# Two column groups instead of one by seven block products in the first channel mixing of batches 2 to 6, six output buffers instead of eight, and a written-out order for every engine

## The chip, the cores and the metric

The kernel runs on one core of a Trainium2 chip. A core has a matrix engine (TensorE, "PE" in the profile; its weight loads are shown apart as "PEld"), a vector engine (VectorE, "DVE"), an engine for activations (ScalarE, "ACT"), a general engine (GpSimd, "POOL") and an engine that here only issues transfers (SyncE, "SP"). Each runs its own list of instructions in order; an instruction that waits for another engine or for a transfer holds up everything behind it on its engine. Products land in PSUM, eight banks of 128 x 512 fp32, from which only DVE and ACT read.

The metric is device time in microseconds, the median of several runs. Before the change it is 247.42 us (three runs, 247.22 to 247.65).

## The reference: what is computed

There are 8 batches of 576 positions, 8 heads of 64, in fp32. Linear attention comes first, and its output, 576 x 512 per batch, goes into a mixer with four weights:

```python
phi = where(x > 0, x, exp(x) - 1) + 1            # applied to q and k
kv  = einsum('bhsd,bhse->bhde', phi(k), v);  z = phi(k).sum(seq)
x   = (phi(q) @ kv) / (phi(q) . z + 1e-6)        # 576 x 512 per batch
h   = relu(x.T @ w_tok1) @ w_tok2                # token mixing, 576 -> 256 -> 576
u   = x + h.T
out = u + relu(u @ w_ch1) @ w_ch2                # channel mixing, 512 -> 1536 -> 512
```

The channel mixing is most of the arithmetic: two products of 576 x 512 x 1536 per batch.

## The kernel before

**Tiles.** The 576 positions of a batch are four row tiles of 128 and a tail of 64; the tails of two batches are mixed together. Work is in bf16, sums and outputs in fp32. The steps of a batch, with their lines: `load` (L132) brings two head pairs of q, k or v (576 KB) into a raw buffer; from batch 2 on there is one raw buffer per tensor. `phi_exp` (L151, ACT), `phi_add` (L157, DVE) and `phi_end` (L165, DVE, a min of the two) make phi; `vcast` (L176) casts v. `kv` (L191) is the k-v product, `nd_all` (L261 on PE, L270 to L289 on DVE) the numerators and denominators. `mm1` (L312) and `mm2` (L325, residual on DVE in L337) are the token mixing. Transposes by DMA (L221 for q, L521 and L526 for u) are issued from SP.

**First channel mixing.** Twelve column groups of 128, each one PSUM bank: `mm3` (L543) makes four products of 512 columns, and ACT applies the Relu (L550; DVE in a few, L547). Groups 4, 5, 10 and 11 of batches 2 to 6 go another way: `mix_one` takes their 512 x 512 block product as seven products of half-size blocks (Strassen's scheme in Winograd's form) instead of eight, each as four products of 256 columns (L712). It needs sums of the weight blocks (`group_sums`, once, L700) and of the blocks of u (`u_sums`, DVE, L689, per batch). Three of the seven are copied out by ACT (L720), three are read by DVE as add-and-Relu (L531), one by ACT as Relu (L718). Batch 7 does all its groups this way (`mix_first`, L740, L746, L748).

**Second channel mixing.** For batches 1 to 6 `pair_product` (L852) makes seven half-size products, after row sums of the first mixing's result (`row_sums`, L655, DVE). `pair_copy` (L857, ACT), `pair_end` (L861 on DVE, L863 on POOL) and `pair_put` (L867) put an output together in four slots of `obuf`, of which there are eight, taken in rotation. Batch 0 uses `mm4` (L583).

**What sets the order.** Each engine runs its instructions in the order in which the code makes them. `run(big, fill)` calls a list of PE steps (`big`: first mixing, second mixing) and, after each, the steps of the next batches that were put at that place by hand (`fill`). So attention and token mixing of batch n+1 lie between the products of batch n, and phi of batch n+2 beside them. PSUM banks come from two rotating rings or from small tables in the functions. SP's order of loads and transposes follows from the same places. A load can be gated on another transfer (`after`): k of batch 1 waits for the first quarter of the first channel weights, the second quarter of the second channel weights waits for the first half of q of batch 1, and q of batch 2 for that quarter. Weights come on POOL's queue.

Of the kernel before, what the change touches and what calls it, by code (L numbers as in the profile page):

```python
# [10 lines left out]
FP32 = mybir.dt.float32  # L11
# [4 lines left out]
EPS = 1e-6  # L16


@with_exitstack
def kernel(  # L20
# [20 lines left out]
    nc = tc.nc  # L41
# [22 lines left out]
    ring = {1: 0, 2: 0}  # L64

    def bank(at=None):
        if at is None:
            at, ring[1] = ring[1], (ring[1] + 1) % 4
        return psum[:, at]

    def banks(at=None):
        if at is None:
            at, ring[2] = 4 + ring[2], (ring[2] + 2) % 4
        return psum[:, at:at + 2]

    def two16():
        return banks().bitcast(BF16).rearrange("p a (t s) -> p a t s", s=128)
# [24 lines left out]
    uTj = [t.rearrange("p r j c -> p (r j c)").rearrange("p (j r c) -> p j r c", j=NDM, r=R) for t in uT]  # L102
    uTt = const("uTt", [128, 2, NDM, 128])
    cr = [const(f"cr{b}", [128, NCH, SM]) for b in range(2)]
    crt = const("crt", [128, NCH, 128])
    obuf = const("obuf", [128, 8, DM], FP32)
    swc = const("swc", [128, 4, 2, 256])
# [31 lines left out]

    live = {}  # L140
    o_at = [0]

    def o_slots(m):
        at = o_at[0] if o_at[0] + m <= 8 else 0
        o_at[0] = (at + m) % 8
        return obuf[:, at:at + m]

    def phi_exp(nm, n, j0, nj):
        f = raw[nm, rb(n)][:, j0:j0 + nj].rearrange("p j f -> p (j f)")
        e = work.tile([128, 2 * TD], BF16, name="e", tag="e", bufs=4)[:, :nj * TD]  # L150
        nc.scalar.activation(out=e, in_=f, func=AF.Exp)  # L151
        live["e", nm, n, j0] = e

    def phi_add(nm, n, j0, nj):
        f = raw[nm, rb(n)][:, j0:j0 + nj].rearrange("p j f -> p (j f)")
        y = work.tile([128, 2 * TD], BF16, name="y", tag="y")[:, :nj * TD]
        nc.vector.tensor_scalar(out=y, in0=f, scalar1=1.0, scalar2=1.0, op0=ALU.add, op1=ALU.max)  # L157
        for j in range(nj):
            live["y", j0 + j] = y[:, j * TD:]

    def phi_end(nm, n, j0, nj):
        c, i = divmod(j0, 2)
        dst = (kp if nm == "k" else qp)[:, c, :, i:i + nj]
        e, y = live["e", nm, n, j0], live["y", j0][:, :nj * TD]
        live["phi"] = nc.vector.tensor_tensor(  # L165
            out=dst.transpose([0, 2, 1, 3]), in0=e.rearrange("p (i t d) -> p i t d", i=nj, t=T),
            in1=y.rearrange("p (i t d) -> p i t d", i=nj, t=T), op=ALU.min)

    def phi(nm, n, c):
        phi_exp(nm, n, 2 * c, 2)  # L170
        phi_add(nm, n, 2 * c, 2)
        phi_end(nm, n, 2 * c, 2)

    def vcast(n, c, copy=nc.scalar.copy):
        js = slice(2 * c, 2 * c + 2)
        copy(out=vs[:, js, :, 0:D],  # L176
             in_=raw["v", rb(n)][:, js].rearrange("p j (t d) -> p j t d", t=T))

    def bank16():
        return bank().bitcast(BF16).rearrange("p (t s) -> p t s", s=128)  # L180
# [3 lines left out]
    def kv(n, cs):  # L184
        b = n % 2
        ps = banks(4 if n > 1 else None)[:, :, 0:2 * D1].rearrange(
            "p a (c e) -> p a c e", c=2)
        for c in cs:
            for t in range(T):
                for a, i in QUARTERS:  # L190
                    nc.tensor.matmul(out=ps[half[i], a, c], lhsT=kp[half[a], c, t, i],  # L191
                                     rhs=vs[half[a], 2 * c + i, t],
                                     start=(t == 0), stop=(t == T - 1))
        cs = slice(cs[0], cs[-1] + 1)
        for i in range(2):
            at = slice(i * D1, (i + 1) * D1)
            nc.scalar.copy(out=kvbd[b][half[i], cs, :, at].transpose([0, 2, 1, 3]),
                           in_=ps[half[i], :, cs])
# [6 lines left out]
    TS = [range(0, 5), range(5, T)]  # L205

    def qtr_put(n, c, ts, tp, put, dst=None):
        v_ = (qT[n % 2] if dst is None else dst)[:, 0:4 * TD].rearrange("p (a c t s) -> p a c t s", a=2, c=2, t=T)
        put(out=v_[:, :, c, ts[0]:ts[-1] + 1].transpose([0, 2, 1, 3]),
            in_=tp[:, 0:len(ts)].rearrange("p t (a s) -> p t a s", a=2))  # L210

    def qtr(n, c, put=nc.scalar.copy):
        tp = two16()
        for h, ts in enumerate(TS):
            qtr_mm(c, ts, tp[:, h])
        for h, ts in enumerate(TS):
            qtr_put(n, c, ts, tp[:, h], put)

    def qtr_dma(n, halves=range(2)):
        for a in halves:  # L220
            live["crossbar"] = nc.sync.dma_start_transpose(  # L221
                out=qT[n % 2][:, 2 * TD * a:2 * TD * (a + 1)].rearrange("p (f s) -> p f s", s=D),
                in_=qp[half[a]].rearrange("p c t i d -> p (c t i d)"))

    def nd_mm(n, c, rs):
        b = n % 2
        ps = banks()
        for s_, r in enumerate(rs):
# [5 lines left out]
        live["nd", c, rs[0]] = ps  # L234

    def nd_end(n, g, rs):
        b = n % 2
        m = len(rs)
        v_ = live["nd", g, rs[0]][:, 0:m, 0:HG * D1].rearrange("p r (h e) -> p r h e", h=HG)
# [9 lines left out]

    def nd_all(n):
        b = n % 2
        ps = [psum[:, 2 + 2 * m:4 + 2 * m] for m in range(3)]
# [10 lines left out]
        xv = x[b].rearrange("p r (c i a d) -> p i (r c) a d", c=2, i=2, a=2)  # L265
        v_ = [ps[m][:, :, 0:D1 * 7].rearrange("p i (k e) -> p i k e", k=7) for m in range(3)]
        dens = work.tile([128, 2, 2, 7], FP32, name="dens", tag="dens", bufs=1)
        last = work.tile([128, 2, 6], FP32, name="dens2", tag="dens2", bufs=1)
        both = psum[:, 2:6, 0:D1 * 7].rearrange("p b (k e) -> p b k e", k=7)
# [4 lines left out]
        def six(m, k0, rc0):  # L274
            den = (dens[:, m] if m < 2 else last)[:, :, k0:k0 + 6]
            nc.vector.tensor_tensor(  # L276
                out=xv[:, :, rc0:rc0 + 3],
                in0=v_[m][:, :, k0:k0 + 6, 0:D].rearrange("p i (q a) d -> p i q a d", a=2),
                in1=den.rearrange("p i (q a) -> p i q a", a=2)[
                    :, :, :, :, None].to_broadcast([128, 2, 3, 2, D]), op=ALU.mult)  # L280

        for m, at in enumerate((6, 0)):
            six(m, m, 4 * m)
            nc.vector.tensor_tensor(
                out=xv[:, :, 3, m], in0=v_[m][:, :, at, 0:D],
                in1=dens[:, m, :, at, None].to_broadcast([128, 2, D]), op=ALU.mult)
        nc.vector.tensor_scalar(out=last, in0=v_[2][:, :, 0:6, D], scalar1=EPS, scalar2=None,
                                op0=ALU.add)
        nc.vector.reciprocal(out=last, in_=last)  # L289
        six(2, 0, 7)  # L290

    def nd(n, g, rs):
        nd_mm(n, g, rs)
        nd_end(n, g, rs)

    ALL = slice(0, DM)
# [9 lines left out]
    def mm1(n):  # L306
        b = n % 2
        ps = banks(4 if n > 1 else None)
        for mt in range(NT):
            ms = slice(128 * mt, 128 * mt + 128)  # L310
            for r in range(R1):
                nc.tensor.matmul(out=ps[:, mt], lhsT=w1t[:, b, ms] if r == R else w1[:, r, ms],  # L312
                                 rhs=x[b][:, r, :], start=(r == 0), stop=(r == R))
        for mt in range(NT):
            nc.scalar.activation(out=ar[b][:, mt, :], in_=ps[:, mt], func=AF.Relu)

    def mm2(n, rs, add=False):

        b = n % 2
        m = len(rs)  # L320
        ps = bank().rearrange("p (a d) -> p a d", a=1) if n == 1 else banks(
            None if n < 2 else 4 if rs[0] else 6)
        for i, r in enumerate(rs):
            for kt in range(NT):
                nc.tensor.matmul(out=ps[:, i], lhsT=w2v(kt, r, b),  # L325
                                 rhs=ar[b][:, kt, :], start=(kt == 0),
                                 stop=(kt == NT - 1 and not add))
            if add:
                nc.tensor.matmul(out=ps[:, i], lhsT=identity, rhs=x[b][:, r, :], start=False,
                                 stop=True)  # L330
        if rs[0] == R:
            h = half[b]
            nc.vector.tensor_tensor(out=ut[n // 2 % 2][h], in0=ps[h, 0], in1=x[b][h, R], op=ALU.add)
        elif add:
            nc.scalar.copy(out=u[b][:, rs[0]:rs[0] + m], in_=ps[:, 0:m])
        else:
            nc.vector.tensor_tensor(out=u[b][:, rs[0]:rs[0] + m], in0=ps[:, 0:m],  # L337
                                    in1=x[b][:, rs[0]:rs[0] + m], op=ALU.add)

    def mm2_tails(p):  # L340

        ps = banks(6)[:, 0]
        for kt in range(NT):
            at = D * (T * kt + 2 * R)
# [966 lines left out]
```

## Time and profile before

| | before |
|---|---|
| median of the runs | 247.42 us |
| profiled execution, first to last instruction | 246.4 us |
| PE busy | 236.1 us (96%) |
| DVE busy | 198.8 us (81%) |
| ACT busy | 139.3 us (57%) |
| POOL busy | 76.9 us (31%) |
| granted PE clock | full in all of the span |

The profiled execution is one run; its span stands 1.0 us below the median of the timed runs. The page counts matmuls as busy from start to modelled end, so that neighbours overlap: what one costs is the distance between starts in the chain of work, not its mean length. A group row reads "line engine operation, out<-in, shapes, count | busy us, mean ns | idle before it, and what ended that idle time". Rows of waits read "engine line <- what it waited for: us in total, times, longest". A row of stages reads from:to, length, then the busy time of PE, PEld, DVE, ACT and POOL with their counts, the granted clock, the share of the DMA engines and the GB/s moved. The times of DMA issues are from issue to landing.

The stages of the execution: batch 0's attention and token mixing to 21.0 us; batch 0's channel mixing, with batch 1's attention inside, to 51.8; batch 1's channel mixing to 85.5; then one stage per batch of about 24 to 25 us (30 for batch 3, which also carries a pair of tails) up to 214.3, and batch 7 to the end.

### The profile page before, as it was taken

The numbers are of one execution on the slowest core, as the hardware profiler recorded it, in microseconds if no ns is written. First come the engines' busy times: TensorE is split into PE (matmuls) and PEld (weight loads), VectorE is DVE, ScalarE is ACT, GpSimd is POOL, SyncE is SP. The second block draws the span as 40 slices with busy tenths as digits, with TensorE's granted clock in tenths as the row PEclk, the third lists the DMA queues.
The fourth block names the chain that finished last, engine by engine and source line by source line (L and its number), as shares of the span: only waits on it lengthen the run. The fifth ranks groups of instructions, "written<-read, shape, count | busy, mean of one in ns | idle before, by whom it ended". The sixth has DMA issues, their size and how long they took to land.

```text
span 246.4 us, 6090 instructions
## 1 busy us (share of the span) xinstructions
PE 236.1 (96%) x2477; PEld 162.3 (66%) x2496; DVE 198.8 (81%) x349; ACT 139.3 (57%) x224; POOL 76.9 (31%) x88
## 2 busy tenths in 40 slices
PE   7789999999999899999999999999999999999993
PEld 3475455564868456865678556865676567888883
DVE  5955877889799998988894499979996779956973
ACT  4673881569774367736897167656852652175100
POOL 9670030296703600061004500071007700440360
PEclk9999999999999999999999999999999999999999
DMA  6999999999726796589979955459748702352055
GB/s 248 267 203 258 348 275 308 355 251 289 294 24 133 223 334 271 132 224 210 358 263 174 412 148 192 93 115 329 228 89 94 170 3 43 64 112 61 4 127 130
DMA packets 50444, 48.40 MB, mean 196 GB/s; under 512 B 30192, under 2 KB 36720, under 8 KB 50416
## 3 DMA queue, kind: packets, MB, share of 16 engines
q1 hardware_dynamic: 41984, 35.00, 48.2%
q0 software_dynamic: 7472, 12.22, 22.7%
q10 hardware_dynamic: 960, 0.79, 1.4%
q8 instruction: 19, 0.31, 0.5%
q14 instruction: 9, 0.07, 0.1%
HBM read 35.85 MB, written 9.44 MB: 184 GB/s over the span
## 4 chain that ended last, share of the span: by engine, by line
PE 84%; DVE 6%; DMA 5%; issue 3%; ACT 1%; SPq 0%; DVEq 0%
PE ps L543 22%; PE ps L852 18%; PE ps L712 6%; PE ps L312 6%; PE ps L583 5%; PE ps L740 4%; PE ps L768 4%; PE ps L325 4%; DMA q_raw<-in_q_dram 3%; PE ps L557 2%; PE ps L570 2%; DMA uT<-u 2%; PE ps L820 2%; PE ps L261 2%; PE ps L191 1%
## 5 line engine op out<-in xcount | busy, mean ns | idle before, releaser
L543 PE MATMUL ps<-uT,wc 128*128 128x512 bf16 x252 | 60.2, 379 | 0.8 <-DMA uT<-u 0.5
L550 ACT ACTIVATE cr<-ps 128x512 bf16<-128x512 f32 x59 | 34.7, 600 | 32.9 <-PE ps L543 32.7
L543 PEld LDWEIGHTS <-wc 128*128 128x128 bf16 x256 | 24.1, 98 | 25.1 <-DMA uT<-u 0.8
L863 POOL TENSOR_TENSOR obuf<-obuf,q_raw 128x512 f32<-128x512 f32 x6 | 8.1, 1344 | 93.3 <-DVE obuf L861 59.1
L852 PE MATMUL ps<-k_raw,v_raw 128*128 128x256 bf16 x216 | 24.9, 273 | 0.0
L852 PEld LDWEIGHTS <-v_raw 128*128 128x128 bf16 x216 | 21.0, 98 | 3.9 <-issue 0.4
L852 PEld LDWEIGHTS <-cr 128*128 128x128 bf16 x216 | 21.1, 98 | 3.7
L861 DVE TENSOR_TENSOR obuf<-ps,u 128x512 f32<-128x512 f32 x24 | 16.3, 685 | 8.1 <-PE ps L852 5.8
L151 ACT ACTIVATE e<-q_raw 128x1152 bf16<-128x1152 f32 x16 | 18.3, 1163 | 7.3 <-DVE x L244 5.5
L151 ACT ACTIVATE e<-k_raw 128x1152 bf16<-128x1152 f32 x16 | 18.2, 1165 | 2.7 <-DMA k_raw<-in_k_dram 2.7
L852 PE MATMUL ps<-wc,cr 128*128 128x256 bf16 x144 | 17.7, 273 | 0.0
L276 DVE TENSOR_TENSOR x<-ps,dens 128x768 bf16<-128x768 f32 x18 | 17.2, 953 | 0.4
L655 DVE TENSOR_TENSOR v_raw<-cr 128x768 bf16<-128x768 bf16 (+2 forms) x24 | 14.8, 617 | 2.1 <-ACT cr L718 2.1
L337 DVE TENSOR_TENSOR u<-ps,x 128x1024 bf16<-128x1024 f32 x12 | 14.6, 1217 | 0.4 <-PE ps L325 0.3
L176 ACT CAST vs<-v_raw 128x1152 bf16<-128x1152 f32 x12 | 13.5, 1161 | 0.0
L312 PE MATMUL ps<-x,w 128*128 128x512 bf16 x49 | 13.0, 379 | 0.3
L165 DVE TENSOR_TENSOR qp<-e,y 128x1152 bf16<-128x1152 bf16 x16 | 11.9, 753 | 1.6 <-ACT e L151 0.9
L165 DVE TENSOR_TENSOR kp<-e,y 128x1152 bf16<-128x1152 bf16 x16 | 12.7, 816 | 0.5 <-ACT e L151 0.4
L157 DVE TENSOR_SCALAR y<-k_raw 128x1152 bf16<-128x1152 f32 x16 | 11.7, 763 | 1.3 <-DMA k_raw<-in_k_dram 1.3
L157 DVE TENSOR_SCALAR y<-q_raw 128x1152 bf16<-128x1152 f32 x16 | 12.4, 793 | 0.4 <-DMA q_raw<-in_q_dram 0.4
L325 PE MATMUL ps<-ar,w2p 128*128 128x512 bf16 x44 | 11.8, 379 | 0.3
L583 PE MATMUL ps<-wc,cr 128*128 128x512 bf16 x47 | 11.9, 379 | 0.1
(182 smaller groups left out, 458.8 us busy)
## 6 DMA issues: line engine op xcount, KB each, us to landing
k_raw<-in_k_dram SPq DMA_DIRECT2D x16, 576.0 KB, 7.6
q_raw<-in_q_dram SPq DMA_DIRECT2D x16, 576.0 KB, 5.9
v_raw<-in_v_dram SPq DMA_DIRECT2D x14, 576.0 KB, 9.2
out_dram<-obuf POOLq DMA_DIRECT2D x12, 512.0 KB, 6.9
wc<-in_moe_w_ch_dram POOLq DMA_DIRECT2D x8, 384.0 KB, 9.8
out_dram<-obuf POOLq DMA_DIRECT2D x4, 256.0 KB, 6.0
out_dram<-obuf ACTq DMA_DIRECT2D x12, 64.0 KB, 2.2
out_dram<-obuf SPq DMA_DIRECT2D x12, 64.0 KB, 1.9
```

The lines of the kernel that those rows point to most:

```text
L151: nc.scalar.activation(out=e, in_=f, func=AF.Exp)
L157: nc.vector.tensor_scalar(out=y, in0=f, scalar1=1.0, scalar2=1.0, op0=ALU.add, op1=ALU.max)
L165: live["phi"] = nc.vector.tensor_tensor(out=dst.transpose([0, 2, 1, 3]), in0=e.rearrange("p (i t d) -> p i t d", i=nj, t=T), in1=y.rearran ...
L276: nc.vector.tensor_tensor(out=xv[:, :, rc0:rc0 + 3], in0=v_[m][:, :, k0:k0 + 6, 0:D].rearrange("p i (q a) d -> p i q a d", a=2), in1=den.r ...
L312: nc.tensor.matmul(out=ps[:, mt], lhsT=w1t[:, b, ms] if r == R else w1[:, r, ms], rhs=x[b][:, r, :], start=(r == 0), stop=(r == R))
L325: nc.tensor.matmul(out=ps[:, i], lhsT=w2v(kt, r, b), rhs=ar[b][:, kt, :], start=(kt == 0), stop=(kt == NT - 1 and not add))
L543: nc.tensor.matmul(out=ps, lhsT=wc1[:, kj, 128 * mc:128 * mc + 128], rhs=uTj[b][:, kj] if n < 2 else uT[b][:, :, kj], start=(kj == 0), sto ...
L550: nc.scalar.activation(out=cr[b][:, mc, :], in_=ps, func=AF.Relu)
L583: nc.tensor.matmul(out=ps, lhsT=crt[:, kc, :] if t == 8 else cr[b][:, kc, 128 * r:128 * r + 128], rhs=wc2[:, kc, :], start=(kc == 0), stop ...
L655: return engine.tensor_tensor(out=s_[which - 1][:, ks], in0=x_, in1=y_, op=op)
L852: nc.tensor.matmul(out=live[tile_][:, j], lhsT=lhs[:, k_], rhs=rhs[:, k_], start=(first and j == 0 and k_ == 0), stop=(k_ == KH - 1), skip ...
L861: nc.vector.tensor_tensor(out=o, in0=live[tile_], in1=u[n % 2][:, d::2, HC[c]], op=ALU.add)
```

## The change

Four things change.

1. In batches 2 to 6 a second set of column groups (2, 3, 8, 9) is made by the seven block products. Four calls of `mm3` per batch go. `swc`, the weight sums, gets a second part for it.
2. `obuf` has six slots instead of eight (`NO`), and each use names its slot (`SLOT`): the outputs of batches 1 to 6 all take slots 0 to 3.
3. The steps are cut finer (products and their reads are steps of their own) and called from one list, `ORDER`. Each engine's order follows from this list. PSUM banks (`BANK`), exp and max buffers (`EBUF`, `YBUF`), the gates of loads (`GATE`) and which reads DVE does (`ON_DVE`) are tables.
4. The row sums 1 and 2 of batches 2 to 6 are cut at weight block 2 instead of 3 (`CUTS`).

Names in `ORDER` begin with the batch: `1kx1` is exp of k's second half, `ka` and `kb` max and min, `L` a load, `v` the cast, `K` the k-v product and `Kc` its copies, `1Q00` a transpose of q on PE, `ma`/`mb` two halves of `mm3` (`m` a whole one) and `r` its Relu, `0q` a step of batch 0's second mixing, `x`/`y` a block product and its read (group, product), `w` row sums, `s` sums of u, `G` weight sums, `p` the second mixing, `e`, `h`, `o` the output. Two places of `BANK` that are spoken of below: groups 2 and 9 of batch 0 share bank 7 (`0m2:7`, `0m9:7`), groups 1 and 6 of batch 4 bank 1 (`4m1:1`, `4m6:1`).

```diff
+NO = 6
+GSW = {2: 0, 1: 1}
+HOLD = {2: 'p0 p1 p2', 1: 's2 s3 s2'}
+CUTS = {1: [0, 3, 6], 2: [0, 2, 6], 3: [0, 2, 6], 4: [0, 2, 6], 5: [0, 2, 6], 6: [0, 2, 6], 7: [0, 2, 4, 6]}
+GATE = {'1k0': ('wc1', 0), '2q0': ('wc2', 1), '4q0': ('u', 2, 1), '7q0': ('u', 5, 1)}
+ON_DVE = {'1v0', '2v1', '0r3', '0r6', '0r9', '1r5', '1r8'}
...
+ORDER = """A2 A0 A1 A3 A4 A5 A6 A7 A8 A9 A10 A12 A13 A14 A11 A15 A19 A16 A17 A20 A18 A21 A22 A23 A24 A25 A26 A27 A28 A29
+A30 A33 A31 A32 A35 A34 A36 1Lk0 A37 1Lk1 A38 A39 1Lq1 A40 1Lq0 A41 1Lv0 1Lv1 A42 A43 0ma1 0ma0 At2 At3 0ma2
+0ma8 1kx0 1ka0 0ma5 0mb5 0ma7 0r5 0mb8 0gt 0r8 0mb7 0gv 1kx1 0mb1 1ka1 0ma4 0ma3 0r7 1kb0 0mb0 0r1 1kb1 0mb2
+0r0 0mb3 0r2 0ma10 1qa1 1qx1 0mb10 G13 0ma11 0r3 0mb11 0mb4 0r11 0ma9 1qa0 1qx0 B0 0mb9 0ma6 B1 0mb6 0r10 1qb0
+0q0 B2 0r4 1v0 1Q00 1Q01 1qb1 1Qc00 0q1 0r9 1Qc01 0q2 1v1 0r6 1Q10 1Q11 1Qc10 1K 2Lq0 ws02 1Qc11 0q3 2Lq1 1Kc1
...
+5qT1 3p60 6ka1 5K 3c1 5qT0
+3p31 5Kc1 6kb1 5Kc0 3p20 4s1 6Lv1 6qa1 3p71 4s2 6v0 3p21 6ka0 3p70 6kb0 7Lv0 U12 7Lk1 3eW 3p30 6qa0 4m0 V1 6v1
+3eZ 3p41 3eY 4r0 3p40 6qx0 3hY 4m1 3eX 5n 4r1 3hW 5nd 4m7 5ne 5n0 3hZ 4m6 4r7 5o0 4x21 5n2 4r6 3o 4x15 6qx1
...
+    obuf = const("obuf", [128, NO, DM], FP32)
+    swc = const("swc", [128, len(GSW), 4, 2, 256])
...
+    def load_in(nm, n, c):
+        gate = GATE.get(f"{n}{nm}{c}")
+        live["in", nm, n, c] = load(nm, n, c, live[gate] if gate else None)
...
+    def group_sums(g, which):
+        s_ = swc[:, GSW[g]]
+        a11, a12, a21, a22 = [cblock(m, h)[:, :, 256 * g:256 * g + 256] for m in range(2) for h in range(2)]
...
+    def mix_mm(n, g, i):
+        first = i in (1, 2, 5)
+        b = n % 2
+        ps = mix_tile(n, g, i)
...
+        for j in range(2):
+            for k_ in range(2):
+                nc.tensor.matmul(out=ps[:, j], lhsT=lhs[:, k_, 128 * j:128 * (j + 1)],
+                                 rhs=rhs[:, :, k_],
+                                 start=(first and j == 0 and k_ == 0), stop=(k_ == 1),
+                                 skip_group_check=not first or j == 1)
+
+    def mix_read(n, g, i):
...
+        if i == 4:
+            nc.scalar.activation(out=dst(1, 0), in_=ps, func=AF.Relu)
+        elif i in (1, 6, 5):
+            nc.scalar.copy(out={1: c1, 6: c6, 5: c5}[i], in_=ps)
+        else:
+            o, c = {2: (dst(0, 0), c1), 3: (dst(0, 1), c6), 7: (dst(1, 1), c5)}[i]
+            add_relu(o, ps, c)
...
+    for name in ORDER.split():
+        tok[name]()
```

## The prediction

> **What bounds the kernel now.** I read the page's totals first, then the chain that ended last in order of time, then the busy time by stage, then who waits for whom.
>
> ```profile
> PE 236.1 (96%) x2477; PEld 162.3 (66%) x2496; DVE 198.8 (81%) x349; ACT 139.3 (57%) x224; POOL 76.9 (31%) x88
> ```
>
> TensorE is the bound: 236.1 of 246.4 us, at full granted clock in all 40 slices. Its 10 us of idle lie almost wholly before the first loads land and in the output tail. A busy PE need not be an efficient one, so the chain gives the true prices, as distances from start to start (start, length, what):
>
> ```profile
> 166.86 1.83 PE ps L543 x8
> 168.69 0.48 PE ps L712 x4
> 169.17 1.73 PE ps L543 x8
> ...
> 172.20 0.87 PE ps L712 x8
> ...
> 184.38 5.18 DMA uT<-u
> ```
>
> Eight 128x512 products (L543, ordinary first mixing) cost 1.73 us, 0.216 each; eight 128x256 products (L712, the block products) 0.87, 0.109 each. The 379 and 273 ns of the group rows are latencies and are no price. By stage (batches 2, 4 and 5 from first mixing to first mixing):
>
> ```profile
> 85.50:109.20 23.70, 23.59 (x269) 16.65 (x272) 21.85 (x37) 15.37 (x24) 4.00 (x5) 1.00 0.76 233
> 139.15:164.40 25.25, 25.15 (x277) 17.15 (x278) 22.75 (x38) 16.47 (x25) 3.97 (x5) 1.00 0.59 171
> 164.40:189.60 25.20, 24.61 (x273) 16.83 (x272) 21.97 (x37) 14.47 (x23) 5.57 (x6) 1.00 0.75 182
> ```
>
> The columns are the length, then PE, PEld, DVE and ACT busy. PE is full; DVE is second with 87 to 92% and 1.9 to 3.2 us of waiting per stage. What PE waits for after the opening is short:
>
> ```profile
> PE ps L261 <- DVE obuf L610: 0.6, 1, 0.6
> PE ps L543 <- DMA uT<-u: 0.5, 1, 0.5
> ```
>
> Last, the loads of batch 1, because the new order leans on them. ACT in the opening, and the one load issued at 18.2 us:
>
> ```profile
> 24.77 0.60 ACT L550 ACTIVATE cr<-ps 128x512 bf16<-128x512 f32 x1
> 25.25 1.17 ACT L151 ACTIVATE e<-k_raw 128x1152 bf16<-128x1152 f32 x1
> 26.61 0.60 ACT L550 ACTIVATE cr<-ps 128x512 bf16<-128x512 f32 x1 [0.19 <-PE ps L543]
> 27.47 0.60 ACT L550 ACTIVATE cr<-ps 128x512 bf16<-128x512 f32 x1 [0.27 <-PE ps L543]
> 28.49 1.16 ACT L151 ACTIVATE e<-k_raw 128x1152 bf16<-128x1152 f32 x1 [0.42 <-DMA k_raw<-in_k_dram]
> 29.56 1.10 ACT L550 ACTIVATE cr<-ps 128x512 bf16<-128x512 f32 x2
> ```
> ```profile
> k_raw<-in_k_dram SPq DMA_DIRECT2D x1, 576.0 KB, 10.2
> ```
>
> The second half of k lands at 18.2 + 10.2 = 28.4, and the exp waits for it although the kernel put five Relu reads ahead of it. Whoever stands behind that exp on ACT waits too.
>
> **The base.** The sum is made against this execution: span 246.4. The median of the runs is 247.42, 1.0 above the span; I add that 1.0 at the end.
>
> **Block products.** Per batch, 16 products of 512 columns go and 28 of 256 come. Five batches: 140 x 0.109 - 80 x 0.216 = 15.3 - 17.3 = **-2.0 us** on PE, which is the path. Bounds: the L712 groups of four cost 0.44 to 0.48, so 0.109 to 0.120: -2.0 to -0.5; I keep -2.0, since most groups are 0.44 or 0.87.
>
> [...]
>
> **DVE and ACT.** Four Relu reads on ACT become three copies and one Relu (600 against about 588 ns): nothing. DVE gains 3 add-and-Relu per batch at 0.688 (row L531; 0.60 start to start), 15 in all, 9.0 to 10.3 us, and four more 128x512 weight sums, 1.7 us at 0.42. The row sums cut at 2 instead of 3 move the same data. In a stage DVE then has 21.85 + 2.0 to 22.75 + 2.0, some 24 to 24.8, where PE needs 23.3 to 24.85. Its cover is gone: before it could idle 1.9 to 3.2 us per stage, now 0 to 0.5. From below the cost is 0, if the new order removes DVE's waits; from above DVE waits as before, +2.0 in each of the stages of batches 2, 4 and 5 (batch 3's stage is 29.95 long with DVE 22.27, and keeps its cover). Following batch 4 by these rows, DVE finishes the first sums about when PE comes to product 5, with under 0.3 us to spare, so I take +0.4 in all, near the lower end.
>
> **Order, opening.** SP issues the batch 1 loads after the same wait (first piece of the first channel weights) and in the same place, only q's halves swapped; POOL's weight loads are the same. So k's halves land at about 24.5 (issue 17.8 + 6.7) and 28.4 again. But ACT now has both exps early: exp, 2 Relu, exp, 4 Relu (groups 7, 1, 0, 2). PE from 21.0: up to the first half of group 9 stand 20 half groups at 0.43, eight transposes 0.45 and one tail product 0.55: 9.6, arrival 30.6. Group 9 takes bank 7 from group 2, whose Relu is fourth behind the exp: 28.4 + 1.07 + 3 x 0.55 + 0.60 = 31.75. PE stops 1.15. Four half groups and the first second-mixing step (1.73 + 0.86) bring it to 34.4, where it transposes q. That needs exp of q's first half, on ACT behind exp of the other half and the Relu of group 11: 31.75 + 1.05 + 0.55 + 1.05 = 34.4, plus DVE's min 0.7: 35.15. Another 0.8. Two transposes and two mixing steps later (2.73) batch 1's k-v product starts at 37.9; in the trace it starts at 36.2: +1.7, and +0.2 for the copy that the next product waits for, **+1.9**. Bounds: 0 if k lands by 27.2, and 2.3 if it comes half a microsecond later. The second channel weights, gated on q's first half (now the fourth load: 32.0 against 30.4), come 1.6 later; at 6.3 from issue to landing they are in time at 38.4, as PE is late itself.
>
> [...]
>
> **Order, later.** Gone, if the order does it: PE's waits of 0.6 (tail output before the batch 3 products) and 0.5 (uT): **-1.1** (0 to -1.4, the idle of those stages). New: by PE's sums, the two v loads of batch 6 are issued 4.2 and 4.1 us before the ACT casts that read them; v landings took 6.3 at the least (median 9.2). Behind the second cast stand the Relus of batch 4's groups 0, 1 and 7. At 6.3 the cast ends at 139.6 on PE's scale, group 1's Relu (behind group 0's and an exp) at 141.8, and PE wants its bank at 140.8: **+1.0** (0 to 4). The k load of batch 6 has 4.1 us, against 3.7, median 7.6, 11.2: **+0.5** (0 to 2.6). u's transpose into batch 6 has 4.7 with a q transpose just ahead; such a pair took 5.2: **+0.3** (0 to 0.5). Two output buffers fewer: every batch now writes the same four; a put lands in 6.9 and the next use is over 15 us away: 0. PSUM banks are named by hand; where a reader is late, I have counted it.
>
> **Sum.** -2.0 + 0.4 + 1.9 - 1.1 + 1.0 + 0.5 + 0.3 = +1.0. Span 247.4, time **248.4**.
>
> **Rivals.** (1) Faster: the loads are in time, as fewer collisions bring k by 27.2 and v within 5.2. Then -2.0 + 0.4 - 1.1 + 0.3 = -2.4: 245.0. For it: PE is the bound and loses work; k landed in 6.7 to 7.0 elsewhere. Against it: the opening's loads meet the same weight loads. (2) Half of it: the opening is lost, the later loads come in time: -0.5, 246.9 to 247.2, about unchanged. (3) DVE becomes the bound: waits of half their old length, +1.0 in three stages, on top of the forecast: 250.9 less the 0.4 counted, 250.5 to 251. For it: no stage has over 0.5 us of cover left. Against: DVE's work can slide between batches. (4) The exchange saves nothing, at 0.120 a product: 249.9.
>
> **Chances.** Forecast (247.5 to 249.6) 0.48; (1) 0.22; (2) 0.13; (3) 0.14; (4) 0.03. A measurement of this kernel tells about 0.2%, 0.5 us, from no change. Faster: (1) and a little of (2), 0.25; same: most of (2) and the forecast's lower edge, 0.14; slower 0.61. Eight in ten: 245.6 to 250.6; the forecast's own range stands above.
>
> **What would show it.** Right: ACT's exp of k in the opening waiting 1 us or more on a DMA, PE waiting for ACT just after 30 us, batch 1's k-v product at 37 or later; PE busy some 2 us lower; DVE near 209 to 211 busy; ACT waiting on a v load near 137 to 140. Wrong: batch 1's k-v product at 36.2 or earlier, or a stage of batch 4 or 5 at 24.7 without DVE or ACT waits behind it.

## The result and the profile after

The changed kernel takes 257.85 us (four runs: 256.37, 256.61, 259.09, 259.84) against 247.38 for the kernel before: a ratio of 1.042 (95% interval 1.036 to 1.048). The prediction was 248.4, with 245.6 to 250.6 as its range. The sign was right; the loss is ten times the forecast one and lies far outside the range.

The profiled execution is the one of 256.37; its span is 254.6. The page's totals and, from the chain, products of 512 and of 256 columns (start, length, what):

```profile
PE 237.6 (93%) x2556; PEld 168.5 (66%) x2556; DVE 207.8 (82%) x368; ACT 137.5 (54%) x224; POOL 78.5 (31%) x88
```
```profile
113.75 0.86 PE ps L675 x4
114.61 2.18 PE ps L917 x20
```

A product of 512 columns (L675) still costs 0.215, one of 256 (L917, a block product) 0.109. PE's price did not move; its idle time did, from 10.3 to 17.0 us. DVE has 9.0 us more to do. By stage, here from the token mixing of one batch to that of the next (batches 3, 4, 5 and 6; the same stages of the kernel before are 25.3, 30.0, 25.2 and 25.4 long; the new order moves products from one stage to another, as their counts show, so only the sums compare: 110.4 us against 105.9):

```profile
94.30:121.90 27.60, 26.55 (x313) 19.75 (x312) 24.50 (x43) 19.20 (x30) 6.02 (x7) 1.00 0.92 262
121.90:152.40 30.50, 27.50 (x317) 19.64 (x315) 25.19 (x43) 18.78 (x28) 4.96 (x5) 1.00 0.92 235
152.40:177.70 25.30, 23.61 (x281) 17.25 (x279) 20.94 (x37) 14.05 (x23) 4.80 (x5) 1.00 0.74 153
177.70:204.70 27.00, 26.67 (x304) 19.59 (x302) 24.52 (x41) 13.27 (x24) 10.93 (x14) 1.00 0.58 129
```

PE is all but full in the last row alone: it has 3.0 us of idle in the second and 1.7 in the third, and DVE idles 5.3 and 4.4 there. In these two no engine sets the pace. Who waits for whom shows what does; first what PE waits for, then ACT, then DVE:

```profile
PE ps L376 <- ACT cr L684: 2.8, 1, 2.8
...
PE ps L959 <- DVE obuf L1051: 1.3, 1, 1.3
PE ps L675 <- ACT cr L684: 0.9, 2, 0.7
PE ps L309 <- DVE qp L251: 0.9, 1, 0.9
PE ps L376 <- DMA qT<-qp: 0.8, 1, 0.8
```
```profile
ACT e L241 <- DMA k_raw<-in_k_dram: 9.6, 6, 2.3
...
ACT vs L264 <- DMA v_raw<-in_v_dram: 7.6, 2, 4.3
```
```profile
DVE y L245 <- DMA k_raw<-in_k_dram: 5.6, 4, 2.0
...
DVE crt L874 <- DMA uT<-u: 4.6, 3, 2.6
```

Before, ACT waited 2.7 us on k and not at all on v, and DVE 1.3 on k and not at all on a transposition of u. From 50 us on, PE's waits of more than 0.15 us add up to 6.6 us, against 1.3 before. The longest of them, and what led to it on the chain:

```profile
146.93 0.36 PE L376 MATMUL ps<-kvbd,qT 64*128 64x65 bf16 x12 [2.78 <-ACT cr L684]
```
```profile
136.58 0.68 SPq L324
...
137.31 2.47 SPq L324
...
139.84 5.32 DMA v_raw<-in_v_dram
...
146.29 0.59 ACT cr L684
146.88 1.05 ACT e L241
147.93 0.50 ACT cr L684
...
148.47 1.02 PE ps L675 x4
```

It begins on SP. The second half of v of batch 6 could have been loaded from 134.4 on, when the cast that last read its buffer ended. It stood behind both transpositions of q of batch 5 (L324) and was issued at 139.84. ACT waited 4.29 us for it, and two Relus and an exp stood behind the cast. PE stopped 2.8 us for the first Relu, that of group 0 of batch 4, because the products of batch 5's numerators and denominators (L376) take its bank (`4m0:6`, `5n2:6` in `BANK`), and 0.2 us more for the second.

The transpositions are the second place. In this trace four of the twelve transpositions of u went out with no load of q, k or v on its way (issued before them and not yet landed): they took 3.1 to 3.3 us from issue to landing. Four had one such load ahead of them and took 3.1 to 5.3 us, and four had two and took 4.1 to 6.6. The slowest, issued at 162.48, is the one that DVE waited 2.6 us for; PE's 1.3 us (L959, at 170.2) stand behind the read that DVE made next.

The opening came much as forecast. ACT there (the last figure in brackets is the idle time before the instruction), then PE:

```profile
28.12 1.16 ACT L241 ACTIVATE e<-k_raw 128x1152 bf16<-128x1152 f32 x1 [1.55 <-DMA k_raw<-in_k_dram]
29.19 2.04 ACT L684 ACTIVATE cr<-ps 128x512 bf16<-128x512 f32 x4
```
```profile
31.28 1.89 PE L675 MATMUL ps<-uT,wc 128*128 128x512 bf16 x8 [0.69 <-ACT cr L684]
...
34.84 0.66 PE L309 MATMUL ps<-identity,qp 128*128 128x128 bf16 x9 [0.81 <-ACT cr L684]
...
37.67 0.78 PE L291 MATMUL ps<-vs,kp 64*64 64x65 bf16 x72
```

The exp waits 1.55 us, PE stops twice, and batch 1's k-v product (L291) starts at 37.7, forecast 37.9, before 36.2.

### The profile page after: what moved, and what is told of

Read it like the earlier page. It is cut to its first block, busy times and chain, and to the rows that moved or that the text cites. A ratio compares the mean times of both kernels' runs of the same rounds, so it can differ in the third digit from the quotient of the medians.

```text
span 254.6 us, 6220 instructions
## 1 busy us (share of the span) xinstructions
PE 237.6 (93%) x2556; PEld 168.5 (66%) x2556; DVE 207.8 (82%) x368; ACT 137.5 (54%) x224; POOL 78.5 (31%) x88
## 4 chain that ended last, share of the span: by engine, by line
PE 61%; DVE 15%; DMA 12%; ACT 5%; issue 3%; SPq 2%; DVEq 0%; ACTq 0%
PE ps L959 14%; PE ps L917 12%; PE ps L675 10%; PE ps L736 5%; PE ps L437 4%; PE ps L448 3%; DMA k_raw<-in_k_dram 3%; DMA q_raw<-in_q_dram 3%; DMA qT<-qp 2%; DVE cr L670 2%; DVE y L245 2%; PE ps L700 2%; DMA v_raw<-in_v_dram 2%; PE ps L722 2%; DMA uT<-u 2%
## 5 line engine op out<-in xcount | busy, mean ns | idle before, releaser
L675 PE MATMUL ps<-uT,wc 128*128 128x512 bf16 x176 | 42.0, 379 | 1.5 <-ACT cr L684 0.9
L1058 POOL TENSOR_TENSOR obuf<-obuf,w 128x512 f32<-128x512 f32 x6 | 7.6, 1265 | 93.4 <-DVE obuf L1051 72.1
L684 ACT ACTIVATE cr<-ps 128x512 bf16<-128x512 f32 x39 | 22.4, 600 | 17.9 <-PE ps L675 17.8
L959 PE MATMUL ps<-k_raw,v_raw 128*128 128x256 bf16 x252 | 31.4, 273 | 0.2 <-ACT q_raw L1045 0.2
L675 PEld LDWEIGHTS <-wc 128*128 128x128 bf16 x176 | 16.5, 98 | 18.9 <-issue 2.9
L959 PEld LDWEIGHTS <-cr 128*128 128x128 bf16 x252 | 24.2, 98 | 6.8 <-issue 2.2
L959 PEld LDWEIGHTS <-v_raw 128*128 128x128 bf16 x252 | 24.5, 98 | 4.3 <-issue 0.7
L959 PE MATMUL ps<-wc,cr 128*128 128x256 bf16 x168 | 21.9, 273 | 0.3 <-DVE cr L670 0.3
L917 PEld LDWEIGHTS <-swc 128*128 128x128 bf16 x160 | 15.6, 98 | 4.3
L917 PEld LDWEIGHTS <-wc 128*128 128x128 bf16 x156 | 15.2, 98 | 3.6 <-issue 0.2
L917 PE MATMUL ps<-crt,swc 128*128 128x256 bf16 x120 | 16.5, 273 | 0.0
L670 DVE CUSTOM_DVE_ANT_0 cr<-ps,v_raw 128x512 bf16<-128x512 f32 x15 | 10.3, 686 | 6.5 <-PE ps L917 4.2
L825 DVE TENSOR_TENSOR v_raw<-cr 128x512 bf16<-128x512 bf16 (+3 forms) x24 | 14.4, 618 | 0.8 <-ACT cr L930 0.4
```

Source lines behind the costliest of these rows:

```text
L670: nc.vector._custom_dve(TENSOR_ADD_SAT, out=o, in0=ps, in1=c, s0=3.4028234663852886e38, s1=0.0)
L675: nc.tensor.matmul(out=bank(f"{n}m{mc}"), lhsT=wc1[:, kj, 128 * mc:128 * mc + 128], rhs=uTj[b][:, kj] if n < 2 else uT[b][:, :, kj], start ...
L684: nc.scalar.activation(out=o, in_=ps, func=AF.Relu)
L917: nc.tensor.matmul(out=ps[:, j], lhsT=lhs[:, k_, 128 * j:128 * (j + 1)], rhs=rhs[:, :, k_], start=(first and j == 0 and k_ == 0), stop=(k_ ...
L959: nc.tensor.matmul(out=ps, lhsT=lhs[:, k_], rhs=rhs[:, k_], start=(first and not skip and k_ == 0), stop=(k_ == KH - 1), skip_group_check= ...
L1058: nc.gpsimd.tensor_tensor(out=o, in0=o, in1=part[i], op=ALU.add)
```

## The experiments

Times are medians; "before" is the kernel before, run beside each on the same chip, 247.4 to 247.7. "Lead" is the time from the issue of a load to the first exp, max or cast that reads it.

**Is it the loads, SP's order or DVE?** Four runs: the changed kernel without the loads of batches 3 to 7, the same for the kernel before, SP's list reordered, and the new add-and-Relu reads given to ACT.

```diff
 # e1_no_loads: ORDER without 3Lk0 ... 7Lv1;  c1_before_no_loads: load_all only for n < 3
 # e4_sp_order: each load as early as its buffer is free, by deadline; two stretches of SP's list
-3qT1 3qT0 4Lq1 2uT1 2uT0 4Lq0 4Lk1 ... 6Lv0 5qT1 5qT0 6Lv1 7Lv0 7Lk1 6qT1 7Lq1 7Lk0
+4Lq1 3qT1 3qT0 2uT1 4Lq0 4Lv0 2uT0 ... 6Lv0 5qT1 6Lv1 5qT0 7Lk1 7Lk0 7Lv0 7Lv1 7Lq1 6qT1
 # e2_relu_act, in mix_read
+            if n < B - 1 and g == 1:
+                nc.scalar.activation(out=o, in_=ps, func=AF.Relu)
```

> The changed kernel without the loads of q, k and v of batches 3 to 7 (their attention is then computed from batch 2's data, which stays in the buffers; everything else is as it was). Theory L (late loads: a load that stands on SP's queue behind a transposition that is still waiting is issued late, and ACT and DVE, which take it in order, hold up PE): the waits of ACT and DVE on k, q and v after 50 us go, and with them most of what was lost between 60 and 215 us, about 6 us: 250 to 253. What stays is the opening (1.6 us) and the tail (1.3 us). Theory D (DVE is the bound with its 15 extra reads): DVE has the same work, so 257 to 258. Theory X (the block products themselves cost PE time): 257 to 258.

> Control to the run without loads: the kernel before, without the loads of q, k and v of batches 3 to 7 (attention of these batches computed from batch 2's data). Its ACT and DVE waited only about 6 us on loads and PE hardly at all, so all theories expect 246.5 to 247.5; if it falls by 3 us or more, taking loads away helps either kernel and the run without loads says nothing on the new order.

> The changed kernel with SP's own list in another order and nothing else moved: loads go ahead of transpositions that wait longer than they (the second v load of batch 6 ahead of a q transposition, the first k load of batch 7 some 16 us earlier, all loads of batches 4, 5 and 7 at the time at which their buffer is free). Theory L: the waits of ACT on v and k of batches 6 and 7 (3.3, 4.3 and 2.0 us) shrink by half or more: 252 to 256. Theories D and X: 257 to 258. If SP's order does not matter because transfers take longer when more are under way, 257 to 258 too, with the landings longer.

> The changed kernel with the three add-and-Relu reads of the new block products of batches 2 to 6 made by ACT as plain Relu reads (the addition of the kept part is left out there, so these column groups are not the reference's). DVE loses 15 instructions of about 0.6 to 0.7 us, 9 to 10 us, and ACT gains 9. Theory D: PE gets what DVE loses, 250 to 254. Theory L: the loads come as late as before and ACT is the one that waits for them, now with more behind it: 256.5 to 259.

Measured: without loads 248.15, its control 248.05, SP's order 257.29, ACT's reads 256.45. Leaving out the loads takes 9.7 us from the changed kernel (my theory L had 5 to 8) and nothing from the one before. So 9.7 of the 10.5 us hang on these loads, and without them the new order is level with the old one. Giving DVE's 15 reads to ACT brought 1.4 us, inside the spread of the two kernels' runs. Moving the loads forward on SP gave only 0.6, against my 2 to 6. The chain of that run shows one reason:

```profile
83.70 5.91 DMA uT<-u
...
90.04 1.29 DVE obuf L1050 x2
91.33 0.04 issue
91.38 0.52 PE ps L375 x12
91.89 5.23 PE ps L674 x12
```

Two loads, issued at 82.73 and 83.19, went out just ahead of this transposition of u. It took 5.9 us, DVE stood 5.3 and PE 4.1, and then twelve products took 5.23 us, 0.436 each, twice their price of 0.215 (see the last section). This profile is of the slowest of the five runs (259.63; the fastest took 256.33).

**One part at a time.** The exchange alone in the hand-made order, six output slots alone, the exchange undone in the new order, and the opening's exp put back.

```diff
 # c2, kernel before: m3x; mixes() calls mix_one(n, g, i) for each pair (g, i)
+mm3 0, 1, 6, 7, then (2,1)(1,1) (1,2)(2,6) (1,6)(2,2) (2,5)(1,5) (2,7)(1,7) (2,3)(1,3) (2,4) (1,4)
 # c3: obuf [128, 6, DM], rotation over 6
 # e3: x11 x16 x17 x14 of batches 2 to 6 become m2 m3 m8 m9, their reads r2 r3 r8 r9
 # e5
-0gv 1kx1 0mb1 1ka1 ... 0r2 0ma10
+0gv 0mb1 ... 0r2 1kx1 1ka1 0ma10 1kb1
```

> The kernel before, in its own hand-made order, with only the exchange: groups 2, 3, 8, 9 of batches 2 to 6 by seven block products too, weight sums in two parts, six output slots, row sums cut at 2. Each old pair of a product of the second set and a whole group gives its place to a pair of block products. Theory L (the exchange is good, the loss of the new order comes from loads): 2.0 us of PE work go and nothing is added on the path: 245.0 to 246.8. Theory D (DVE becomes the bound with 15 more reads, in three stages): 247.5 to 250.5. Theory X (the block products save nothing on PE): 247.3 to 248.5.

> The kernel before with six output slots instead of eight, taken in the same rotation, and nothing else. All theories but one expect 247.2 to 247.8. Theory S (a batch's output waits for the put of the batch before out of the same slots): 248.5 or more, with DVE or POOL waiting on a transfer out of the output buffer.

> The changed kernel, in its new order, with the exchange undone: groups 2, 3, 8, 9 of batches 2 to 6 by ordinary products again, each in the place of one of the block products, with its read on ACT. DVE loses 15 reads. Theory L: the late loads and their waits stay, PE has 2.0 us more: 257.5 to 260. Theory D: with DVE relieved the loss goes, 250 to 254. Theory X (block products cost): 254 to 256.5.

> The changed kernel with one step of the opening moved: ACT's exp of the second half of k of batch 1 (and DVE's max and min of it) stands behind the Relus of groups 7, 1, 0 and 2 again instead of ahead of them. If the opening's loss is what the prediction said (the Relus stand behind an exp that waits for k at 28.4), batch 1's k-v product starts at 36.0 to 36.7 instead of 37.74 and the time falls by 1.0 to 1.6: 256.2 to 256.9. If later waits take it back (the loads of later batches are issued and land when they do), the k-v product comes earlier all the same and the time stays at 257.4 to 258.

Measured: 256.32, 247.56, 256.86, 257.45. (In the first, batch 6's second mixing and in the third some of the undone groups share PSUM banks with live tiles, so these outputs are not the reference's and PE can wait for other banks; the products are the same in number.) Six slots cost nothing in the hand-made order. Undoing the exchange in the new order gives PE its 2.0 us of work back and the time does not rise (1.0 lower, within the spread of both): with the transfers as they are, the exchange brings nothing. That PE's work alone is free there is not shown, as the run also takes 15 reads from DVE. The opening's mend worked in its place, k-v product at 36.9 instead of 37.7, and was taken back at once:

```profile
38.53 1.02 PE L735 MATMUL ps<-wc,cr 128*128 128x512 bf16 x4 [0.82 <-DMA wc<-in_moe_w_ch_dram]
```

The second channel weights are gated on q's first half, which the new order loads second; the prediction had them in time only "as PE is late itself".

The surprise is the exchange alone in the hand-made order: 8.7 us slower, though no load there has a lead under 10 us.

**Which loads; DVE in the hand-made order.** The eleven loads with leads under 8 us left out, the 19 others left out; the exchange alone with mended banks, and the same with its 15 add-and-Relu reads on ACT.

```diff
 # e6: without 5Lk1 5Lk0 5Lq0 5Lv0 6Lk1 6Lk0 6Lq1 6Lv0 6Lv1 7Lk0 7Lv1; e7: without the 19 others
 # c2b: pair_product's banks X 2, Z 0 for n == 6; c4: and Relu on ACT for g == 1
```

> The changed kernel without those eleven loads that are issued less than 8 us before ACT or DVE first want their data (five halves of batch 6, four of batch 5, two of batch 7; the attention of these batches then uses older data); the 19 others of batches 3 to 7 stay. Theory L, short leads: they hold nearly all of the 9.7 us that leaving out all 30 gave, so 248.5 to 250.5. Theory T (traffic: the transfers slow the transpositions and each other): the gain goes with the bytes, 11 of 30, so 253.5 to 255. Theory F (any late load pushes the next ones back, so half measures gain little): 255 to 257.

> The counterpart: the changed kernel without the 19 loads of batches 3 to 7 that are issued 8 us or more ahead (their batches then use older data), while the eleven short ones stay. Theory L: 256 to 258. Theory T: 19 of 30 of the gain, 251 to 252.5. Theory F: between, 253 to 256, as the short ones come earlier on SP's queue with fewer loads ahead of them.

> The kernel before in its hand-made order with the exchange of groups 2, 3, 8, 9 alone, as in the run with the exchange alone, but batch 6's second mixing keeps the PSUM banks that it had, so that nothing writes into them before they are read. The former gave 256.3, with DVE at 209 us busy and no load issued less than 10 us ahead of its use, so loads are not its trouble: 255.5 to 257 by theory D (in this order DVE is late, by some 2 us in each stage); 246 to 248 if the loss was that of the banks.

> The kernel with the exchange alone in the hand-made order, with the three add-and-Relu reads per batch of the second set made by ACT as plain Relu reads (the addition of the kept part is left out in these groups). DVE is relieved of the 15 reads that the exchange added. Theory D for the hand-made order: most of the loss of 8.8 us goes, 246 to 250. If the loss comes from the order in which I set the block products (each waits for the copy of the one before it), it stays: 254 to 257.

Measured: 251.62, 252.50, 256.21, 252.23. Without the short leads 6.2 of the 9.7 us go, without the long ones 5.4: both groups count, the short ones about twice as much per load, and no theory has it alone. In the hand-made order, relieving DVE brings 4.0 of 8.8 us: there rival (3), DVE, is real. The other half was not settled; that it lies in the sequence in which I set the block products is only argued. In that run ACT has these reads to do instead.

**Waits or traffic; what the exchange is worth; can order mend it.**

```diff
 # e8, for n > 2: exp, max and v cast read wc1, as fp32, instead of raw
 # e9: e1 with x11 x12 x15 x14 as m2 m3 m8 m9 in the banks of the block products
 # f1: SP's list, and three moves elsewhere
-4qT0 3uT0 5Lv1 3uT1 4qT1 5Lk1 3ut 5Lk0 5Lq0 6Lk1 6Lk0 5Lv0 6Lq0 4uT0 6Lq1 4uT1 6Lv0 5qT1 5qT0 6Lv1 7Lv0 7Lk1
+5Lq0 5Lk1 4qT0 4qT1 3uT0 3uT1 5Lk0 5Lv0 5Lv1 3ut 6Lv0 6Lk1 6Lk0 6Lv1 6Lq1 4uT0 4uT1 6Lq0 5qT1 5qT0 7Lk1
-5kx1 5qx1 5qx0 5kx0 6kx0 6kx1 5v0 5v1      # ACT
+5kx1 5qx1 5v0 5qx0 5kx0 5v1 6kx0 6kx1
-7D710 7p41 7R31 7D310 7D311 7D711
+7D710 7D711 7p41 7R31 7D310 7D311
 # f1a: SP's list alone (v of batch 6 after 4uT1)
```

> The changed kernel with all its loads, but from batch 3 on exp, max and the v cast read a fixed region of the first channel weights instead of the loaded data (so these batches' attention is computed from weights). Nobody waits for these loads any more; they still take the transfer engines and stand on SP's queue, some a little earlier, as they no longer wait for readers of their buffers. Theory W (what costs is that ACT and DVE wait for loads): 248 to 250. Theory T (what costs is that loads in flight slow the transpositions, 5.3 us for q and 4.3 for u from issue to landing against 3.8 and 3.3 without loads): 254 to 257. Leaving out the short leads gave 6.2 us and leaving out the long ones 5.3 of the 9.7, so I expect a share of each: 250 to 253.

> The changed kernel without the loads of batches 3 to 7 (as in the run without loads, 248.15) and with the exchange undone: groups 2, 3, 8, 9 of batches 2 to 6 by ordinary products, each in the place and in the bank of one of the block products. With no load to wait for, this prices the exchange in the new order. By PE's prices, 140 products of 0.109 us against 80 of 0.216: 2.0 us slower, 249.8 to 250.5. If DVE's 15 extra reads cost in the new order as they do in the hand-made one, it is faster than 248.15.

> The changed kernel with the two causes mended by order alone, nothing left out: on SP no load stands behind a transposition that waits longer than it, and none is issued just ahead of one that is about to be issued and is soon needed; ACT casts v of batch 5 some 10 us earlier, so that v of batch 6 can be loaded earlier, and makes the exps of k of batch 6 a few us later; one put at the end is issued one place earlier. If short leads and collisions hold the loss, most of the 9.7 us comes back: 249 to 252. If the late loads are only a sign of something else (DVE, banks, the exchange), 256 to 258.

> The changed kernel with SP's list alone in the mended order: loads no longer behind transpositions that wait longer, and none issued just ahead of a transposition of u that is soon needed; ACT's and DVE's lists as in the changed kernel. Against the first reordering of SP's list (257.3), which differs in that it put two loads just ahead of the transposition of u of batch 2 and others ahead of that of batch 4. If collisions with the transpositions of u hold most of the loss, 250.5 to 253; if the short leads of v and k of batch 6 (which this order cannot mend) hold most, 254 to 257.

Measured: 254.71, 250.84, 249.88 and 253.61. With nobody waiting for the loads of batches 3 to 7, 6.6 of the 9.7 us stay lost, more than I expected (250 to 253) and in the range of theory T: loads can cost that much with nobody waiting for their data. (ACT and DVE read the first channel weights there, as PE does; what that costs is not tested.) SP there, then its chain:

```profile
154.47 0.64 SPq L216 DMA_DIRECT2D q_raw<-in_q_dram  x1
155.16 0.50 SPq L216 DMA_DIRECT2D k_raw<-in_k_dram  x1
156.75 1.24 SPq L484 DMA_TRANSPOSE uT<-u  x1
158.08 0.53 SPq L216 DMA_DIRECT2D v_raw<-in_v_dram  x1
158.66 3.04 SPq L484 DMA_TRANSPOSE uT<-u  x1
```
```profile
158.66 8.15 DMA uT<-u
...
166.90 0.09 DVE crt L880
...
167.98 2.72 PE ps L965 x12
```

A transposition of u with three loads just ahead of it took 8.15 us; DVE (which forms the sums of u from it) stood still for 4.5 us and then PE for 2.3. Order alone, with all work kept, brings 8.0 us back (f1): SP's list 4.2 of them (f1a, between the ranges of the two theories), and the rest comes from the earlier casts of v, the later exps of k, the earlier loads of v that they allow, and one put at the end. And without loads the exchange is worth 2.7 us.

| kernel | us | leads under 8 us, of 30 | median lead | uT, issue to landing | qT |
|---|---|---|---|---|---|
| before | 247.4 | 0 | 13.5 | 3.1 | 3.7 |
| changed | 257.85 | 11 | 10.3 | 4.3 | 5.3 |
| loads read by nobody (e8) | 254.7 | - | - | 4.6 | 5.5 |
| SP by deadline (e4) | 257.3 | 3 | 15.7 | 3.6 | 5.2 |
| SP mended (f1a) | 253.6 | 5 | 13.7 | 3.3 | 4.4 |
| SP and ACT mended (f1) | 249.9 | 3 | 13.7 | 3.4 | 5.6 |

The table warns against taking the lead for the cause. SP by deadline and SP and ACT mended have three short leads each and are 7.4 us apart, and the former has the longer median lead; its order cures the late issues (the median load leaves 0.6 us after its buffer is free, not 5.0) and puts loads ahead of transpositions.

**A version that is level or better.** f1's trace still had PE waiting 0.8 us for a Relu behind the exp and 0.5 us for the gated weights in the opening, and 0.7 us at 113.5 for a copy behind the cast of v. f2 mends these and two puts at the end together; how much each brings is not shown.

```diff
 # f2 = f1 and
-    live["in", "q", 1, 0] if i == 1 else None)     # gate of the second weights
+    live["in", "q", 1, 1] if i == 1 else None)
-(nc.sync, nc.scalar)[b].dma_start(                 # tail_put
+(nc.gpsimd if i == 7 else (nc.sync, nc.scalar)[b]).dma_start(
 # and in ORDER: e5's move; 5v0 behind 5qx0
 # f3 = f2 with 0r4 ahead of 0r10
```

> The version with mended loads (249.88), with three more places mended by order: in the opening, ACT's exp of the second half of k of batch 1 behind the four Relus again, and the second quarter of the second channel weights gated on that half of q of batch 1 which is loaded first (the third load, not the fourth; in the run with the opening alone mended, PE waited 0.8 us for these weights where the time had been won); the cast of v of batch 5 one exp later, so that it no longer stands ahead of a copy that PE waits for at 113.5 (0.7 us); two puts of the tails at the end from POOL's queue instead of SP's and ACT's. If these are the places where it still loses: opening 1.3 to 1.8, cast 0.5 to 0.7, puts 0.3 to 0.7, so 246.8 to 248.0, level with the kernel before. If other waits take them back, 248.5 to 250.

> The version that is level with the kernel before (247.18), with ACT's Relu of group 4 of batch 0 ahead of that of group 10: the transposition of q of batch 1 on PE takes group 4's bank and waited 0.6 us for it. If that wait is all, 246.6 to 246.9; if PE then waits for q's phi instead (0.9 us of it is there already), 247.0 to 247.4.

Measured: f2 247.18, a ratio of 0.9985 (0.9968 to 1.0002), level with the kernel before; f3 247.09 against 247.52 beside it, 0.9981 (0.9968 to 0.9993). The swap's gain, 0.1, is inside the spread; the 0.6 us that PE waited for the Relu became a longer wait for q's phi. Its waits of PE, the longest of the start (L1078) aside:

```profile
PE ps L308 <- DVE qp L250: 1.2, 2, 0.7
PE ps L735 <- DVE cr L681: 0.4, 1, 0.4
```

So with these moves the exchange and the new order together are worth about 0.2% (0.07 to 0.32 by f3's interval), and as the change has them they cost 4.2%.

## Why the prediction was wrong

- **Block products, -2.0: right in price.** 0.215 and 0.109 in the trace after; the exchange is worth 2.7 us with the loads left out. But it was booked on a path that PE did not set: with the loads in place, undoing it cost nothing.
- **DVE, +0.4: not contradicted, and too small to be shown.** Giving the reads to ACT brought 1.4 us, inside the spread. The mechanism, DVE without cover, is real in the hand-made order, where the same 15 reads hold 4.0 us.
- **Opening, +1.9: right in mechanism, and near in size.** The k-v product started at 37.7 (forecast 37.9), 1.5 later than before.
- **Gone waits, -1.1: mostly came.** The wait on u went, and of the 0.6 on the tail output 0.3 was left (L675, at 87.4). But other waits came (6.6 us after 50 us, above).
- **Order, later, +1.0 +0.5 +0.3: the step that failed.** It holds that late transfers cost 1.8 us; leaving the loads out shows 9.7, where 7.1 was the sum of my upper bounds. The place of the worst single wait was right (v of batch 6, ACT near 140, Relus behind the cast), though PE stopped for group 0's bank, not for group 1's as forecast. Three errors made the price. First, I gave the transpositions 0.3 us in all, with 5.2 us at most for one, the trace's pair behind one another. Those of u took up to 6.6 us with loads on their way in the changed kernel, against 3.1 to 3.3 with none, and 5.9 and 8.2 behind loads in two of the runs. This error looks the largest, as 6.6 us of time stay lost when nobody waits for the loads themselves. Second, I took each load as issued on PE's scale and added only its landing time (in the trace before, the loads issued from SP took 3.3 to 14.7 us from issue to landing). What its place on SP's list adds I did not count: the second load of v of batch 6 left 5.5 us after its buffer was free, behind two transpositions of q, and the median load of batches 3 to 7 left 5.0 us after. Third, I priced three loads, those with the shortest leads on paper; in the trace eleven of 30 had under 8 us, where the kernel before has none. How the 9.7 us divide between the first error and the other two in the changed kernel itself stays open, as the experiments move both together.
- **Tail: left out.** From the last DVE read's start to the end 5.1 us instead of 3.7, with three puts still to be issued by ACT after it, where there was one: 1.4.

Summed with what the runs showed: 9.7 for transfers, 1.5 opening, 1.4 tail, -2.7 exchange make 9.9 of the 10.5 us. These terms come from different runs; the run without loads fits them (1.5 + 1.4 - 2.7 = 0.2, measured 0.1 above its control).

Of the signs that the prediction named, those of the opening and ACT's wait for v near 140 came. PE's busy time did not fall by 2 us but rose by 1.5, though a product's price held, and DVE was 207.8 us busy, not 209 to 211. In rival (3) the prediction's sum is off: three stages at +1.0 on 248.4, less 0.4, make 251.0, the upper end of its range.

A transposition of u took 8.15 us behind three loads (loads read by nobody), against a median of 3.3 in the run without loads. That is a reason to ask what stands ahead of each transposition; I asked it of one pair of transpositions and not of loads.

## What to carry to other kernels

When an order is redrawn, list for each transfer three times: when its buffer is free, when its queue reaches it, and when its data are first wanted; compare the shortest leads with those of the kernel before (8.7 us there, 4.6 here), since a late load holds up more than its own reader: here ACT waited 4.3 us for v of batch 6, and PE 2.8 us for a Relu behind that cast. But good leads are not enough, as SP by deadline shows: look for what is issued just ahead of a small transfer that is soon needed: in that run a transposition of u issued just behind two loads took 5.9 us, against 3.1 to 3.3 for those with none on their way in the changed kernel. And price the removal of work only after asking what sets the pace once it is gone: here an exchange that saves 2 us of PE work was worth nothing until the transfers were in time.

## What the runs showed of the hardware

A short stop of PE can be followed by a stretch at half clock, in which products cost twice their price. With SP's list by deadline PE waited 4.1 us, to 91.4; the page has the granted clock at 5 tenths in the slice from 90.2 to 96.7 us, and the twelve products of 512 columns behind the wait cost 0.436 us each, against 0.215. With the loads read by nobody it waited 2.3 us, to 168.0; the granted clock (the column after the counts) stood at half for 3.4 us, and the first twelve products of 256 columns cost 0.227 each (2.72 us), against 0.109:

```profile
160.00:167.80 7.80, 5.65 (x52) 4.91 (x51) 3.29 (x6) 4.97 (x7) 0.00 (x0) 1.00 1.19 216
167.80:171.20 3.40, 3.22 (x34) 2.14 (x35) 2.91 (x6) 0.00 (x0) 0.83 (x1) 0.50 0.23 89
171.20:180.00 8.80, 8.80 (x85) 6.13 (x80) 8.48 (x17) 5.85 (x11) 8.49 (x12) 1.00 0.41 88
```

It does not follow every wait. After the 2.8 us wait in the profile of the changed kernel, to 146.9, the clock was full (1.00 in the stages from 121.9 to 177.7); the mean of that profile, 0.994, comes from its end, 0.97 from 248.0 to 252.0 us and 0.50 from there to 254.6. The exchange alone and its repeat have the same longest wait, 2.1 us, and mean clocks of 0.993 and 0.999. SP mended and the exchange undone, with longest waits of 2.6 and 2.4 us, have 0.993 too; where the clock fell in these spans is not shown. What such a stretch costs in all is not shown either. The two longer runs of the changed kernel (259.1 and 259.8) have a mean clock of 0.988 and 0.990 where the two shorter have 0.994 and 0.998, so it may be part of their 2.5 to 3.5 us. But of the runs with loads read by nobody, 253.70 us had a mean clock of 0.999, 253.75 (the one above) 0.989 and 255.86 again 0.998: there the time does not follow the clock.

Issuing is not free either: in the run with loads read by nobody a load held SP for 0.5 to 0.6 us between 151 and 165 us, a transposition for 1.2 to 3.1.
